# Two more PSUM banks for the hidden products of a two-layer MLP, and new due times for its weight conversions

## The chip, the cores and the metric

The kernel runs on one core of one Trainium2 chip. The metric is device time in microseconds (us), the median of several executions; one more execution is recorded by the hardware profiler, and the rows below come from it.

## The reference, cut to what matters

Attention with mixed heads gives `x` of 1792 tokens x 768; two layers follow it, and the change lies mostly in them:

```
h = x @ moe_w_in             # 1792 x 2048
g = s * relu(h)**2 + b
x = g @ moe_w_out            # 1792 x 768
h = x @ moe2_w_in
g = h * cos(h)
out = g @ moe2_w_out
```

All of it is float32. The kernel splits each operand into a high part that the fast matmul format holds exactly and a low rest, and adds three products: high x high, high x low, low x high.

## The kernel before, in words

**A plan, and then in-order queues.** The program is first a list of steps. Each step has a due position `pos`, an engine, a cost, steps it comes after, and tiles that it takes or uses. `Plan.run` walks through planned time: an engine that is free takes the step with the smallest `pos` that is ready and whose tiles are free in the plan. The order that comes out is the order in which each engine's instructions are written. On the chip every engine runs its own list in that order and waits at an instruction until its semaphores are up. So a due time or a cost changes no work, only the order on the queues of PE, DVE, ACT, POOL and SP.

**The attention** runs first. Per tile it does on PE the mix `p` (lines 457 to 459), then a maximum on DVE (468), the exponential `e` on ACT (475), weights `w` on DVE (488), the second mix `a` on PE (498) and its copy `at`. For each of eight half batches three pairs of products `vps` (535) with the values follow; they are copied to `xo` and stored to `x` in DRAM. `AVC` is the cost that the plan gives to one of the 48 steps of `vps`.

**The layers.** A layer's 2048 hidden columns are cut into eight slices of 256 (`f`), a slice into two halves of 128 (`c`). The tokens are cut into four blocks `j` of 512, 512, 256 and 512. A unit is a slice with a token block. `hidden` makes the 18 products of a half into one PSUM bank `h` (line 778 before, 779 after), `output` adds the unit's share of `g @ w_out` through PSUM banks `o` (line 841 in layer 1, 869 in layer 2; 842 and 870 after) into `acc` in SBUF (line 848 and 878 on DVE). PE's due order is: hidden of unit u+1, then output of unit u. In layer 2 a unit's output is made in blocks of 128 tokens, two banks and 12 products a block.

**What holds a hidden bank.** In layer 2 a half's bank is read by ACT (`ta`, 807), written and read again by DVE and ACT as scratch (811, 813, 815), and read last by the sine on ACT (`tb<-h`, 816). Only then may PE start another half in this bank. Before, there are two such banks (`ph`, one per half), and six for the output (`po`).

**Weights.** Each of a slice's four weight tiles (`weight(n, c, o)`: input weights `wi` with o=0, output weights `wo` with o=1) is loaded as float64 in two pieces, and each piece is split on ACT (700, 720), DVE (702, 707, 709, 714, 724) and POOL (726, 728) into `wh` and `wl`. The due times of these steps are given from `a`, the due time of the second unit of the slice before. `TOK` and `WT0` are the same for the tokens (`tokens`, 753 and 754) and the first slice's weights; `TAIL` places the layers behind the attention.

Of the kernel before, what the change touches and what calls it, by code (L numbers as in the profile page):

```python
# [10 lines left out]
F32 = mybir.dt.float32  # L11
# [6 lines left out]
PSUM = bass.MemoryType.PSUM  # L18
# [547 lines left out]
SHI = 16  # L566
OFF = (4.214, 4.208, 3.018, 2.518, 2.061, 1.245)
AVP = (2.713, 3000.0)
AVC = 900.0
W1 = (-1.242, 4.569)  # L570
W2 = (-1.416, 6.158)
W3 = (2.491, 1.454)
# [2 lines left out]
def mlp(pl, tc, x, w1, wo1, s, b, w2, wo2, out, left, right, psl, psr, bank, room, room_free, stored, gates, t_start):  # L575
# [6 lines left out]
    NF = DFF // 256  # L582
# [5 lines left out]
        t0 += n  # L588
    NB = len(TB)
    before_right, before_psr, before_left = gates  # L590
    for name, cap in (("raw2", 2), ("cm", 2), ("ca", 2), ("ce", 2), ("wi", 3), ("wo", 4), ("ta", 2), ("tb", 2), ("g0", 2), ("g1", 2), ("ph", 2), ("po", 6)):
        pl.ring(name, cap)
    P = {}

# [2 lines left out]
    for j in (0, 1):  # L597
        for z in range(2):
            for k in range(KD):
                n = TB[j][1]  # L600
# [35 lines left out]
    def open_left():  # L636
        left.close()
        psl.close()
        pool = lambda name, bufs=1: left.enter_context(tc.tile_pool(name=name, bufs=bufs, reuse_waits="tile"))
        P["po"] = psl.enter_context(tc.tile_pool(name="m_po", bufs=6, space=PSUM, reuse_waits="tile"))  # L640
        P["g"], P["wo"], xp = pool("m_g", 2), pool("m_wo", 4), pool("m_y")
        for j in (2, 3):
            for z in range(2):
                xx[z, j] = xp.tile([128, KD, TB[j][1]], F32R, name=f"x{z}{j}")
        for j in range(NB):
            acc[j] = xp.tile([128, KD * TB[j][1]], F32, name=f"acc{j}")
# [3 lines left out]
    g_psr = pl.add(t_start - 20000, "none", 0, open_psr, behind=before_psr)  # L650
    g_left = pl.add(t_start, "none", 0, open_left, behind=before_left + [g_right, g_psr])
# [8 lines left out]
    units = [(st, f, j) for st in range(2) for f in range(NF) for j in ((0, 1, 3, 2) if (st, f) == (1, NF - 1) else range(NB))]  # L660
    seq = [(st, f) for st in range(2) for f in range(NF)]
    cyc = lambda n: n / 2.4 + 13.5
# [11 lines left out]
    wt, w_done = {}, {}  # L674
# [85 lines left out]
    def hidden(u):  # L760
        st, f, j = u
        n = TB[j][1]
        nn = seq.index((st, f))
        for c in range(2):
            first = u == units[0]
            ring, tag = ("ps", "s") if first else ("ph", "h")
            hp = pl.hold(ring)
            p = at_h[u] + c * 18 * cyc(n)
            hw = wt[nn, c, 0]
            a = None  # L770
            for z in range(3):
                def prod(z=z, hp=hp, hw=hw, first=first, tag=tag):
                    if z == 0:
                        hp.tile = (bank if first else P["ph"]).tile([128, 512], F32, tag=tag, name="h")[:, :n]
                    for k in (2 * z, 2 * z + 1):
                        wh, wl = hw.tile[0][:, k], hw.tile[1][:, k]
                        for y, (w, z_) in enumerate(((wh, 0), (wh, 1), (wl, 0))):
                            nc.tensor.matmul(out=hp.tile, lhsT=w, rhs=cols(z_, j, k)[:, 0], start=(k == 0 and y == 0), stop=(k == KD - 1 and y == 2))  # L778
                xd = x_done[j][2 * z:2 * z + 2] if st == 0 else x_done[1, j]
                a = pl.add(p + z * 6 * cyc(n), "pe", 6 * cyc(n), prod, w_done[nn, c, 0] + xd + [a] + ([] if first else [g_psr]), take=[] if z else [hp], use=[hw])  # L780
            h_first.append(a)
            hg, h1, h2 = pl.hold(f"g{c}"), pl.hold("ta"), pl.hold("tb")
            gt[u, c] = hg
            p += 18 * cyc(n)
            act = n * .84 + 52
            dve = n * 1.05 + 66
            dp = 1000.0

            def open_t(h, tag):
                h.tile = P["t"].tile([128, 512], F32, tag=tag, name=tag)[:, :n]  # L790
                return h.tile

            def open_g(hg=hg, c=c):
                hg.tile = [P["g"].tile([128, 512], F32R, tag=f"{z}{c}", name=z)[:, :n] for z in ("gh", "gl")]
                return hg.tile[0]
            if st == 0:
                a = pl.add(p, "act", act, lambda h1=h1, hp=hp, open_t=open_t: nc.scalar.activation(out=open_t(h1, "ta"), in_=hp.tile, func=AF.Relu), [a], take=[h1], use=[hp])
                if first:
                    early.append(a)
                a = pl.add(p + dp, "dve", dve + 64, lambda h1=h1, h2=h2, open_t=open_t: nc.vector.scalar_tensor_tensor(  # L800
                    out=open_t(h2, "tb"), in0=h1.tile, scalar=P["sc"][:, 0:1], in1=h1.tile, op0=ALU.mult, op1=ALU.mult), [a] + c_sb, take=[h2], use=[h1], port=True)
                a = pl.add(p + 2 * dp, "act", act + 90, lambda h2=h2, open_g=open_g: nc.scalar.activation(
                    out=open_g(), in_=h2.tile, func=AF.Identity, bias=P["sc"][:, 1:2]), [a, g_left], take=[hg])
                a = pl.add(p + 3 * dp, "dve", dve + 64, lambda h2=h2, hg=hg: nc.vector.scalar_tensor_tensor(
                    out=hg.tile[1], in0=h2.tile, scalar=P["sc"][:, 1:2], in1=hg.tile[0].bitcast(F32), op0=ALU.add, op1=ALU.subtract), [a], use=[h2], port=True)
            else:
                a = pl.add(p, "act", act, lambda h1=h1, hp=hp, open_t=open_t: nc.scalar.activation(out=open_t(h1, "ta"), in_=hp.tile, func=AF.Copy), [a], take=[h1])
                a = pl.add(p + dp, "dve", n * .52 + 69, lambda h1=h1, h2=h2, open_t=open_t: nc.vector.tensor_scalar(
                    out=open_t(h2, "tb"), in0=h1.tile, scalar1=1.0 / (2 * math.pi), scalar2=MAGIC, op0=ALU.mult, op1=ALU.add), [a], take=[h2], port=True)
                a = pl.add(p + 2 * dp, "act", act + 90, lambda h2=h2: nc.scalar.activation(out=h2.tile, in_=h2.tile, func=AF.Identity, bias=P["cb"][:, 1:2]), [a])  # L810
                a = pl.add(p + 3 * dp, "dve", dve, lambda h1=h1, h2=h2, hp=hp: nc.vector.scalar_tensor_tensor(
                    out=hp.tile, in0=h2.tile, scalar=-C1, in1=h1.tile, op0=ALU.mult, op1=ALU.add), [a], port=True)
                a = pl.add(p + 4 * dp, "dve", dve, lambda h2=h2, hp=hp: nc.vector.scalar_tensor_tensor(
                    out=hp.tile, in0=h2.tile, scalar=-C2, in1=hp.tile, op0=ALU.mult, op1=ALU.add), [a])
                a = pl.add(p + 5 * dp, "act", act, lambda hp=hp: nc.scalar.activation(out=hp.tile, in_=hp.tile, func=AF.Abs), [a])
                a = pl.add(p + 6 * dp, "act", act + 90, lambda h2=h2, hp=hp: nc.scalar.activation(  # L816
                    out=h2.tile, in_=hp.tile, func=AF.Sin, scale=-1.0, bias=P["cb"][:, 0:1]), [a], use=[hp])
                a = pl.add(p + 7 * dp, "pool", n * 2.4 + 100, lambda h1=h1, h2=h2: nc.gpsimd.tensor_tensor(out=h2.tile, in0=h1.tile, in1=h2.tile, op=ALU.mult), [a], use=[h1])  # L818
                a = pl.add(p + 8 * dp, "act", act + 40, lambda h2=h2, open_g=open_g: nc.scalar.activation(out=open_g(), in_=h2.tile, func=AF.Copy), [a], take=[hg])
                a = pl.add(p + 9 * dp, "dve", dve, lambda h2=h2, hg=hg: nc.vector.tensor_tensor(out=hg.tile[1], in0=h2.tile, in1=hg.tile[0].bitcast(F32), op=ALU.subtract), [a], use=[h2], port=True)  # L820
            g_done[u, c] = a
# [61 lines left out]
    for n in range(len(seq)):  # L883
        if n == 0:
            for i, (c, o) in enumerate(((0, 0), (1, 0), (0, 1), (1, 1))):
                weight(0, c, o, t_start + WT0[i], t_start + WT0[i] + 6000)
            continue
        prev = [at_h[u] for u in units if u[:2] == seq[n - 1]]
        a = prev[1]
        weight(n, 0, 0, a, a + 12000)  # L890
        weight(n, 0, 1, a + 12000, a + 24000)
        weight(n, 1, 0, prev[3] + 18 * cyc(512), prev[3] + 18 * cyc(512) + 9000)
        weight(n, 1, 1, prev[3] - 8000, prev[3] + 3000)
    h_first = []
    for j in (0, 1):
        tokens(j, t_start + TOK[j][0], TOK[j][1])
    for i, u in enumerate(units):
        if u == units[2]:
            for j in (2, 3):
                tokens(j, t_start + TOK[j][0], TOK[j][1])  # L900
        hidden(u)
# [14 lines left out]
        pl.run()  # L916


TOK = ((-16000.0, 3835.4), (-1854.7, 2701.8), (6127.9, 1261.9), (11457.4, 1085.7))
WT0 = (-11637.0, -9965.5, 3371.0, 3000.0)  # L920
TAIL = 13954.5

# [1 line left out]
_INS = ["q", "k", "v", "w_pre", "w_post", "moe_w_in", "moe_w_out", "moe_s", "moe_b", "moe2_w_in", "moe2_w_out"]  # L924
# [23 lines left out]
```

## Time and profile before

| | |
|---|---|
| median of 3 executions | 1492.1 us (1489.51 to 1493.28) |
| profiled execution | 1494.0 us, span of its instructions 1492.2 us |
| PE busy | 1437.1 us, 96% of the span |
| DVE, ACT, POOL busy | 1210.2, 765.7, 626.4 us |
| attention until its last mix `p` ends | to 515.57 us |
| layer 1, first output to last hidden product before layer 2 | 557.83 to 994.16 us |
| layer 2, from its second hidden unit | 1002.34 to 1487.77 us |

The span is what the profile's instructions cover; the profiled time is 1.8 us longer than it. PE is busy nearly all the time, so what is to be read is where it is idle, and where its granted clock is below 1.00.

### The profile page before, as it was taken

Reading aid. Unit: us, or ns where it says so; the run is one execution under the profiler, and the core shown is the slowest. Engines: PE = TensorE matmul, PEld = TensorE weight load, DVE = VectorE, ACT = ScalarE, POOL = GpSimd, SP = SyncE. Lnnn points to the kernel's source line nnn. Section 1 sums busy time; section 2 is a strip of 40 time slices with the busy share of each in tenths; the row PEclk is TensorE's granted clock in tenths of the full one; section 3 lists DMA queues with packets and bytes.
Section 4 is the critical chain, followed back from the end, with each engine's and each line's share of the span. In section 5 each row is a group of like instructions: output and inputs, shape, how many; then the busy total and the mean of one; then the engine's idle time right before and its main releaser. Section 6 shows DMA issues by size and latency. Waiting matters only on the chain.

```text
span 1492.2 us, 23095 instructions
## 1 busy us (share of the span) xinstructions
PE 1437.1 (96%) x8292; PEld 1247.8 (84%) x8292; DVE 1210.2 (81%) x2212; ACT 765.7 (51%) x1595; POOL 626.4 (42%) x548
## 2 busy tenths in 40 slices
PE   6899999999999899999999999999999999999998
PEld 5788888887888778888888888889889898898988
DVE  4777777877877879898877877899899888988855
ACT  4766676666766746332323322357645445454532
POOL 2544454444444534443332333324454454454521
PEclk9999999999999999999999999999999999999999
DMA  6744464463454442221211212111211111111103
GB/s 175 159 129 134 110 157 129 133 144 109 126 128 132 138 135 74 75 64 54 74 45 51 64 43 64 43 46 50 64 54 43 54 53 54 53 44 53 54 30 118
DMA packets 140860, 129.19 MB, mean 87 GB/s; under 512 B 72171, under 2 KB 128459, under 8 KB 140747
## 3 DMA queue, kind: packets, MB, share of 16 engines
q1 hardware_dynamic: 140747, 127.73, 30.3%
q8 instruction: 65, 1.06, 0.3%
q14 instruction: 48, 0.39, 0.1%
HBM read 77.99 MB, written 11.01 MB: 60 GB/s over the span
## 4 chain that ended last, share of the span: by engine, by line
PE 85%; DMA 5%; DVE 4%; ACT 2%; issue 2%; SPq 1%; POOL 1%; DVEq 0%; POOLq 0%; ACTq 0%
PE h L778 30%; PE o L841 16%; PE o L869 15%; PE a L498 7%; PE vps L535 5%; DMA m<-s 3%; PE p L457 2%; PE sps L379 2%; PE sps L380 2%; PE p L459 2%; PE p L458 2%; PE tk L302 1%; PE tq L339 1%; DMA qn<-in_q_dram 1%; DVE w L488 1%
## 5 line engine op out<-in xcount | busy, mean ns | idle before, releaser
L726 POOL TENSOR_TENSOR cm<-ca,wh 128x384 f32<-128x384 f32 x128 | 168.6, 1319 | 387.8 <-ACT wh L720 387.8
L452 POOL TENSOR_TENSOR m<-m,mh 120x448 fp32r<-120x448 f32 x180 | 207.5, 1156 | 207.6 <-ACT mh L447 205.2
L778 PE MATMUL h<-m,wh 128*128 128x512 f32 x672 | 220.4, 398 | 12.4 <-ACT tb L816 12.4
L498 PEld LDWEIGHTS a<-w,e 120*128 120x128 f32 x1440 | 185.1, 194 | 21.0 <-PE p L459 6.5
L498 PE MATMUL a<-w,e 120*128 120x120 f32 x1440 | 189.8, 279 | 9.5 <-DVE w L488 9.5
L778 PE MATMUL h<-x,wh 128*128 128x256 f32 (+1 forms) x768 | 190.2, 339 | 2.2 <-DVE x L754 2.2
L728 POOL TENSOR_TENSOR wl<-cm,ce 128x384 fp32r<-128x384 f32 x128 | 150.2, 1175 | 70.3 <-DVE ce L724 64.6
L778 PEld LDWEIGHTS h<-m,wh 128*128 128x128 f32 x672 | 126.8, 191 | 42.3 <-ACT tb L816 15.6
L778 PE MATMUL h<-m,wl 128*128 128x512 f32 x384 | 152.0, 396 | 0.0
L778 PEld LDWEIGHTS h<-x,wh 128*128 128x128 f32 x768 | 131.9, 188 | 20.2 <-DVE x L754 2.6
L841 PE MATMUL o<-gl,wh 128*128 128x512 f32 (+1 forms) x384 | 140.1, 365 | 0.0
L841 PE MATMUL o<-gh,wh 128*128 128x512 f32 (+1 forms) x384 | 140.0, 365 | 0.0
L841 PE MATMUL o<-gh,wl 128*128 128x512 f32 (+1 forms) x384 | 140.0, 365 | 0.0
L475 ACT ACTIVATE e<-p,st 120x448 f32<-120x448 f32 x180 | 113.9, 633 | 36.8 <-DVE st L468 35.2
L778 PE MATMUL h<-x,wl 128*128 128x512 f32 (+1 forms) x384 | 130.0, 338 | 0.0
L468 DVE TENSOR_REDUCE st<-p 120x1 f32<-120x448 f32 x180 | 110.3, 615 | 23.3 <-PE p L459 22.9
L818 POOL TENSOR_TENSOR tb<-ta,tb 128x512 f32<-128x512 f32 (+1 forms) x64 | 76.0, 1187 | 118.1 <-ACT tb L816 111.6
L447 ACT ACTIVATE mh<-m 120x448 fp32r<-120x448 f32 x151 | 87.2, 577 | 66.1 <-PE p L458 43.9
L720 ACT ACTIVATE wh<-ca 128x384 fp32r<-128x384 f32 x128 | 66.0, 521 | 96.5 <-DVE ca L709 71.8
L878 DVE TENSOR_TENSOR acc<-acc,o 128x384 f32<-128x384 f32 x196 | 100.6, 544 | 17.3 <-PE o L869 17.1
L869 PE MATMUL o<-wh,gh 128*128 128x384 f32 x448 | 113.8, 334 | 0.0
L869 PE MATMUL o<-wh,gl 128*128 128x384 f32 x448 | 113.8, 334 | 0.0
(99 smaller groups left out, 3255.6 us busy)
## 6 DMA issues: line engine op xcount, KB each, us to landing
m<-s SPq DMA_DIRECT2D x144, 192.5 KB
raw<-in_moe_w_in_dram SPq DMA_DIRECT2D x64, 384.0 KB
raw<-in_moe_w_out_dram SPq DMA_DIRECT2D x64, 384.0 KB
qn<-in_q_dram SPq DMA_DIRECT2D x72, 110.0 KB
m<-s SPq DMA_DIRECT2D x36, 210.0 KB
v<-in_v_dram SPq DMA_DIRECT2D x28, 192.0 KB
out_dram<-acc SPq DMA_DIRECT2D x14, 384.0 KB
rk<-in_k_dram SPq DMA_DIRECT2D x18, 224.0 KB
```

The source lines that it names most:

```text
L447: nc.scalar.activation(out=hh.tile, in_=src().bitcast(F32), func=AF.Copy)
L452: a2 = pl.add(p - OFF[1] * STEP, "pool", 1110, lambda hh=hh, src=src: nc.gpsimd.tensor_tensor(out=src(), in0=src().bitcast(F32), in1=hh.ti ...
L468: nc.vector.tensor_reduce(out=hst.tile[:, 0, z:z + 1], in_=hp.tile, axis=AX, op=ALU.max, negate=True)
L475: nc.scalar.activation(out=he.tile, in_=hp.tile, func=AF.Exp, bias=hst.tile[:, 0, z:z + 1], accum_out=hst.tile[:, 1, z:z + 1])
L498: nc.tensor.matmul(out=ha.tile[:, c * L:(c + 1) * L], lhsT=he.tile[:, j:j + 128], rhs=hw2.tile[:, z], start=True, stop=True)
L726: a = pl.add(p0 + 6 * dp, "pool", 1050, lambda hm=hm, ha=ha, flat=flat: nc.gpsimd.tensor_tensor(out=hm.tile, in0=ha.tile.bitcast(F32), in1 ...
L728: got.append(pl.add(p0 + 7 * dp, "pool", 1050, lambda hm=hm, he=he, flat=flat: nc.gpsimd.tensor_tensor(out=flat(1), in0=hm.tile, in1=he.ti ...
L778: nc.tensor.matmul(out=hp.tile, lhsT=w, rhs=cols(z_, j, k)[:, 0], start=(k == 0 and y == 0), stop=(k == KD - 1 and y == 2))
L818: a = pl.add(p + 7 * dp, "pool", n * 2.4 + 100, lambda h1=h1, h2=h2: nc.gpsimd.tensor_tensor(out=h2.tile, in0=h1.tile, in1=h2.tile, op=ALU ...
L841: nc.tensor.matmul(out=hp.tile, lhsT=w, rhs=x, start=(c == 0 and y == 0), stop=(c == 1 and y == 2))
L869: nc.tensor.matmul(out=hp[e].tile, lhsT=x, rhs=w[:, e * HD:(e + 1) * HD], start=(c == 0 and y == 0), stop=(c == 1 and y == 2))
L878: got.append(pl.add(p, "dve", 470, lambda e=e, hp=hp, view=view: nc.vector.tensor_tensor(out=view(), in0=view(), in1=hp[e].tile, op=ALU.ad ...
```

## The change

```diff
-AVC = 900.0
+AVC = 1750.0
...
-("ph", 2), ("po", 6)):
+("ph", 2), ("pi", 2), ("po", 4)):
...
-        P["po"] = psl.enter_context(tc.tile_pool(name="m_po", bufs=6, space=PSUM, reuse_waits="tile"))
+        P["po"] = psl.enter_context(tc.tile_pool(name="m_po", bufs=4, space=PSUM, reuse_waits="tile"))
+        P["pi"] = psl.enter_context(tc.tile_pool(name="m_pi", bufs=2, space=PSUM, reuse_waits="tile"))
...
-            ring, tag = ("ps", "s") if first else ("ph", "h")
+            ring, tag = ("ps", "s") if first else ("ph", "h") if units.index(u) % 2 else ("pi", "i")
...
-        hp.tile = (bank if first else P["ph"]).tile([128, 512], F32, tag=tag, name="h")[:, :n]
+        hp.tile = (bank if first else P[ring]).tile([128, 512], F32, tag=tag, name="h")[:, :n]
...
-   w_done[nn, c, 0] + xd + [a] + ([] if first else [g_psr]), take=[] if z else [hp], use=[hw])
+   w_done[nn, c, 0] + xd + [a] + ([] if first else [g_psr] if ring == "ph" else [g_left]), take=[] if z else [hp], use=[hw])
...
-        weight(n, 0, 0, a, a + 12000)
-        weight(n, 0, 1, a + 12000, a + 24000)
-        weight(n, 1, 0, prev[3] + 18 * cyc(512), prev[3] + 18 * cyc(512) + 9000)
-        weight(n, 1, 1, prev[3] - 8000, prev[3] + 3000)
+        for i, (c, o) in enumerate(((0, 0), (0, 1), (1, 0), (1, 1))):
+            weight(n, c, o, a + WN[n > NF][i][0], a + WN[n > NF][i][1])
...
-TOK = ((-16000.0, 3835.4), (-1854.7, 2701.8), (6127.9, 1261.9), (11457.4, 1085.7))
-WT0 = (-11637.0, -9965.5, 3371.0, 3000.0)
-TAIL = 13954.5
+TOK = ((-16000.0, 1599.1), (-1854.7, -4153.7), (6127.9, -940.2), (11457.4, 2394.5))
+WT0 = (-11637.0, -6972.4, 3371.0, 1170.1)
+TAIL = 13826.2
+WN = (((500.1, 12000.0), (12000.0, 24676.0), (35989.2, 45236.9), (26000.0, 31685.4)), ((979.7, 12000.0), (11251.3, 24000.0), (32000.0, 39901.4), (20648.0, 31850.6)))
```

The output gives up two of its six banks. They become a second pair for the hidden products: even units (token blocks 0 and 2) use `pi`, odd ones `ph`. No product, conversion or load is added or taken away; the plan orders them anew. The order of three places matters below.

ACT, layer 2, around the turn from one slice to the next; before, `h_13488` is the second half of the last unit of a slice and `h_13569` the first half of the first unit of the next:

```order
L720 ACTIVATE wh_13520<-ca_13576 128x384
L807 ACTIVATE ta_13605<-h_13569 128x512
L815 ACTIVATE h_13488<-h_13488 128x512
L816 ACTIVATE tb_13560<-h_13488,cb_5760 128x512
L700 ACTIVATE cm_13631<-raw_13609 128x384
L819 ACTIVATE gh_13633<-tb_13560 128x512
```

The sine of `h_13488` stands behind the copy of `h_13569`. The same place after the change; `h_13396` and `h_13481` are the two halves of the last unit, `h_13567` is the first half of the next slice:

```order
L816 ACTIVATE h_13396<-h_13396 128x512
L817 ACTIVATE tb_13532<-h_13396,cb_5760 128x512
L820 ACTIVATE gh_13604<-tb_13532 128x512
L721 ACTIVATE wh_13550<-ca_13586 128x384
L808 ACTIVATE ta_13609<-h_13567 128x512
L701 ACTIVATE cm_13621<-raw_13577 128x384
L816 ACTIVATE h_13481<-h_13481 128x512
L817 ACTIVATE tb_13537<-h_13481,cb_5760 128x512
```

The sine of the first half now stands ahead of the copy of `h_13567`; that of the second half still stands behind it.

PE at the same turn, before: the end of `h_13569` and the start of the second half of the same unit, whose bank is that of `h_13488`:

```order
L778 MATMUL h_13569<-m_117,wh_13053 128x512 x2
L778 MATMUL h_13569<-m_117,wl_13054 128x512
L778 MATMUL h_13569<-m_117,wh_13053 128x512 x2
L778 MATMUL h_13569<-m_117,wl_13054 128x512
L778 MATMUL h_13617<-m_117,wh_13520 128x512 x2
L778 MATMUL h_13617<-m_117,wl_13521 128x512
```

After, behind `h_13567`:

```order
L779 MATMUL h_13567<-m_117,wh_13082 128x512 x2
L779 MATMUL h_13567<-m_117,wl_13083 128x512
L779 MATMUL h_13597<-m_117,wh_13082 128x512 x2
L779 MATMUL h_13597<-m_117,wl_13083 128x512
L779 MATMUL h_13597<-m_117,wh_13082 128x512 x2
```

Behind the first half of unit 0 there now comes `h_13597`, the first half of unit 1 with the same weights, in the bank of `h_13396`; the second half of unit 0 follows it, in a bank of the other pair.

PE where the attention ends, before: the last mix `p`, the last two pairs of `a`, the products `vps`, and the first hidden half `h_6180`:

```order
L459 MATMUL p_6070<-m_117,wp_h_114 120x448
L498 MATMUL a_6083<-w2_6075,e_6033 128x120 x4
L498 MATMUL a_6093<-w2_6075,e_6046 128x120 x4
L498 MATMUL a_6122<-w2_6116,e_6067 128x120 x4
L498 MATMUL a_6130<-w2_6116,e_6098 128x120 x4
L535 MATMUL vps_6143<-at_118,v_119 64x220 x16
L535 MATMUL vps_6167<-at_118,v_119 64x220 x8
L778 MATMUL h_6180<-m_117,wh_5914 128x512 x2
```

After, from the last mix on:

```order
L459 MATMUL p_6075<-m_117,wp_h_114 120x448
L498 MATMUL a_6093<-w2_6086,e_6032 128x120 x4
L498 MATMUL a_6099<-w2_6086,e_6053 128x120 x4
L779 MATMUL h_6107<-m_117,wh_5906 128x512 x2
L779 MATMUL h_6107<-m_117,wl_5907 128x512
L779 MATMUL h_6107<-m_117,wh_5906 128x512 x2
L779 MATMUL h_6107<-m_117,wl_5907 128x512
L779 MATMUL h_6107<-m_117,wh_5906 128x512 x2
L779 MATMUL h_6107<-m_117,wl_5907 128x512
L779 MATMUL h_6107<-m_117,wh_5906 128x512 x2
L779 MATMUL h_6107<-m_117,wl_5907 128x512
L498 MATMUL a_6139<-w2_6136,e_6073 128x120 x4
```

Twelve of the 18 products of the first hidden half have moved in between the last two pairs of `a`.

## Rows read from the trace of the kernel before

**Rows 1.** The page: busy time, share of the span, instructions

```profile
PE 1437.1 (96%) x8292; PEld 1247.8 (84%) x8292; DVE 1210.2 (81%) x2212; ACT 765.7 (51%) x1595; POOL 626.4 (42%) x548
```

**Rows 2.** Waits of PE, whole span: us in total, times, longest

```profile
PE h L778 <- ACT tb L816: 12.4, 7, 2.3
PE a L498 <- DVE w L488: 9.5, 15, 2.1
```

**Rows 3.** Busy time by window: a slice of layer 1, then three of layer 2

```profile
core 0: us, PE busy (x) PEld busy (x) DVE busy (x) ACT busy (x) POOL busy (x), PEclk, DMA share, GB/s
786.89:844.86 57.97, 57.97 (x290) 49.11 (x289) 46.30 (x81) 17.36 (x32) 19.11 (x16) 1.00 0.18 55
1184.57:1245.02 60.45, 58.55 (x313) 53.61 (x313) 52.37 (x100) 30.26 (x56) 30.09 (x24) 1.00 0.18 53
1245.02:1307.07 62.05, 60.15 (x313) 54.73 (x313) 54.76 (x102) 30.44 (x56) 30.70 (x24) 0.97 0.17 52
1429.58:1487.77 58.19, 58.19 (x325) 54.93 (x323) 33.36 (x63) 21.39 (x38) 9.22 (x8) 1.00 0.21 83
```

**Rows 4.** The same view, sum over the eight slices of layer 2

```profile
sum 485.43, PE 472.99 PEld 432.02 DVE 409.47 ACT 246.23 POOL 218.34; mean PE 59.12 PEld 54.00 DVE 51.18 ACT 30.78 POOL 27.29
```

**Rows 5.** Chain that ended last, around 1300 us: start, us, what

```profile
1290.87 4.19 PE o L869 x24
1295.06 4.14 PE h L778 x18
...
1299.22 0.60 ACT ta L807
1299.82 0.50 ACT h L815
...
1300.34 0.70 ACT tb L816
...
1301.08 5.99 PE h L778 x18
```

**Rows 6.** Timeline of ACT before that wait

```profile
1299.22 0.60 ACT L807 ACTIVATE ta<-h 128x512 f32<-128x512 f32 x1 [2.90 <-PE h L778]
```

**Rows 7.** Windows of PE from two such waits on: us, busy, clock

```profile
1238.70:1245.02 6.32, 4.42 (x20) 1.00 0.15 53
1299.20:1307.07 7.87, 5.99 (x19) 0.78 0.15 50
```

**Rows 8.** Output of one unit of layer 2: chain of PE, timeline of DVE

```profile
1213.66 8.33 PE o L869 x48
...
1216.43 1.00 DVE L878 TENSOR_TENSOR acc<-acc,o 128x384 f32<-128x384 f32 x2
...
1219.55 1.93 DVE L878 TENSOR_TENSOR acc<-acc,o 128x384 f32<-128x384 f32 x4
```

**Rows 9.** Timeline of POOL: last conversion of a slice's second input weights

```profile
1237.34 1.02 POOL L728 TENSOR_TENSOR wl<-cm,ce 128x384 fp32r<-128x384 f32 x1 [0.56 <-DVE ce L724]
```

**Rows 10.** Windows of PE where the attention ends: us, busy, clock

```profile
515.57:519.65 4.08, 2.02 (x17) 1.00 0.70 238
519.65:523.95 4.30, 3.63 (x16) 0.60 0.51 175
553.36:557.83 4.47, 2.29 (x15) 0.94 0.28 87
557.83:567.46 9.63, 9.63 (x37) 0.85 0.29 83
```

**Rows 11.** Chain and waits at the same place

```profile
528.63 2.95 PE h L778 x12
...
571.67 8.16 PE o L841 x36
...
PE h L778 <- DVE x L754: 2.2, 2, 1.1
```

**Rows 12.** Windows in the attention: two with `vps`, one between

```profile
90.00:130.00 40.00, 39.42 (x304) 32.87 (x303) 30.98 (x62) 26.14 (x59) 15.44 (x16) 1.00 0.45 126
160.00:190.00 30.00, 30.00 (x233) 24.47 (x232) 22.02 (x48) 16.30 (x38) 11.96 (x11) 1.00 0.50 119
190.00:215.00 25.00, 22.50 (x149) 19.30 (x149) 17.68 (x37) 17.86 (x43) 11.81 (x11) 1.00 0.64 161
```

**Rows 13.** Chain in the attention: one group of `vps`

```profile
96.84 1.70 PE vps L535 x16
```

More of the change, by code (lines that the diff above doesn't have):

```diff
@@ L590, in mlp @@
     before_right, before_psr, before_left = gates
-    for name, cap in (("raw2", 2), ("cm", 2), ("ca", 2), ("ce", 2), ("wi", 3), ("wo", 4), ("ta", 2), ("tb", 2), ("g0", 2), ("g1", 2), ("ph", 2), ("po", 6)):
+    for name, cap in (("raw2", 2), ("cm", 2), ("ca", 2), ("ce", 2), ("wi", 3), ("wo", 4), ("ta", 2), ("tb", 2), ("g0", 2), ("g1", 2), ("ph", 2), ("pi", 2), ("po", 4)):
         pl.ring(name, cap)
@@ L771, in hidden, with prod @@
             for z in range(3):
-                def prod(z=z, hp=hp, hw=hw, first=first, tag=tag):
+                def prod(z=z, hp=hp, hw=hw, first=first, ring=ring, tag=tag):
                     if z == 0:
-                        hp.tile = (bank if first else P["ph"]).tile([128, 512], F32, tag=tag, name="h")[:, :n]
+                        hp.tile = (bank if first else P[ring]).tile([128, 512], F32, tag=tag, name="h")[:, :n]
                     for k in (2 * z, 2 * z + 1):
@@ L779, in hidden @@
                 xd = x_done[j][2 * z:2 * z + 2] if st == 0 else x_done[1, j]
-                a = pl.add(p + z * 6 * cyc(n), "pe", 6 * cyc(n), prod, w_done[nn, c, 0] + xd + [a] + ([] if first else [g_psr]), take=[] if z else [hp], use=[hw])
+                a = pl.add(p + z * 6 * cyc(n), "pe", 6 * cyc(n), prod, w_done[nn, c, 0] + xd + [a] + ([] if first else [g_psr] if ring == "ph" else [g_left]), take=[] if z else [hp], use=[hw])
             h_first.append(a)
```

## The prediction

> **What bounds the kernel now.** I read the page's busy line first: PE is busy 1437.1 us, 96% of the span, and the next engine, DVE, 81% [rows 1]. So a change that takes no work from PE can at most take back PE's idle time, 1492.2 - 1437.1 = 55 us, and what a granted clock below 1.00 makes its work longer. Second, the waits of PE: two lines matter, hidden products that wait for the sine on ACT (7 times, 12.4 us), and mixes `a` that wait for weights from DVE (15 times, 9.5 us) [rows 2]. Third, windows by stage say where these stand. A slice of layer 1 has no idle time at all: 57.97 us, all of it busy, clock 1.00. Slices of layer 2 take 60.45 and 62.05 us, and the last one, which has no turn to a next slice in it, 58.19 [rows 3]. Over the eight slices of layer 2 the sum is 485.43 us, of which PE is busy 472.99 [rows 4]: 12.4 us idle, which is all of the waits for the sine. A slice at full clock holds 58.55 us of work [rows 3], eight of them 468.4; the other 472.99 - 468.4 = 4.6 us are work at a lower clock. So layer 2 holds 17.0 us that are not work, and layer 1 nothing.
>
> **Why PE waits there.** The chain at 1300 us shows the loop: PE ends the first half of unit 0 of the new slice (18 products, 4.14 us), then ACT makes `ta` (0.60), a second pass (0.50) and the sine `tb` (0.70), and only then PE starts the second half [rows 5]. The sine reads the bank that this half wants, the one of the last unit's second half. It could have run before, but in ACT's list it stands behind `ta` of the new unit, and ACT itself was idle for 2.90 us waiting for PE to end that half [rows 6]. ACT waits for PE, then PE for ACT: 0.60 + 0.50 + 0.70 and a few hundredths, 1.90 us in the window from 1238.70 (6.32 - 4.42) and 1.88 in that from 1299.20 (7.87 - 5.99) [rows 7].
>
> The second effect is in the same two windows. After the first wait the products take 4.42 us at clock 1.00, after the second 5.99 at 0.78 (some of it at the lower level): 1.57 us more. 4.6 / 1.57 is about 3, so about three of the seven waits are followed by such a fall.
>
> **The change in layer 2: the turn.** In the new order the bank that PE asks for behind the first half of unit 0 is that of the last unit's first half, whose sine stands ahead of `ta` in ACT's list; ACT can run it while PE makes the 4.14 us of unit 0. The bank of the second half, whose sine still stands behind `ta`, is asked for only another 18 products or more later; 0.60 + 0.50 + 0.70 = 1.8 us is covered by 4.14. The second half of unit 0 goes to the other pair. So no order is left in which both engines wait for each other, and I take the whole loss back: -12.4 of waits, and -4.6 of clock, since in the windows of before the clock falls only behind a wait: **-17.0**. At worst nothing comes back (0).
>
> What is late next? The second half's weights `wl`: POOL ends the last conversion at 1237.34 + 1.02 = 1238.36, 0.34 us before PE would have asked for them without its wait (1238.70) [rows 9]. With the old due times the removed wait would soon meet this one. Now that half is asked for 18 products later (+4.1 us), and its conversions are also due earlier. I cost it at nothing; with that cover gone it is at most the old wait less the 0.34 us, 1.6 us a turn or 11 in all.
>
> **Four output banks.** A block of an output takes two banks and 12 products, so four banks hold two blocks: the third block waits until DVE has added the first. In the trace of before one unit's 48 products take 8.33 us from 1213.66, 2.08 a block; blocks start at 1213.66, 1215.74, 1217.82 and 1219.91. The adds of the first block end at 1216.43 + 1.00 = 1217.43, 0.4 us before the third block; those of the second are two of the four that start at 1219.55, so they end at about 1220.5, 0.6 after the fourth would start [rows 8]. Six banks hide this, four do not, if DVE keeps this order. In the new order of PE there are three places per slice where only one block lies between two users of a bank; elsewhere hidden products stand between. The bounds are 0 (DVE's list is written anew with four banks known, and DVE has 58.55 - 52.37 = 6.2 us to spare per slice [rows 3]) and 3 x 0.6 = 1.8 us a slice, 14 in all. I take a quarter, 0.45 a slice, because of the three places only the kind of the fourth block is late in these rows, and the spare time exceeds the lateness threefold: 8 x 0.45 = **+3.6**. For layer 1 I take 0: DVE has 57.97 - 46.30 = 11.7 us to spare there [rows 3]; its upper bound is the same +3.6. And since PE never waits in layer 1, extra hidden banks can give it nothing.
>
> **From the attention to layer 1.** Windows show PE idle 4.08 - 2.02 = 2.06 us behind the last `p`, then 4.30 - 3.63 = 0.67, and 2.18 us in the first output; and 16 products that take 3.63 us at clock 0.60, against 2.02 for 17 at 1.00, 1.6 more; then 9.63 us at 0.85 for 37 [rows 10] where a full output of 36 takes 8.16 [rows 11], 1.4 more. In all 2.06 + 0.67 + 2.18 + 1.6 + 1.4 = 7.9 us. The change puts 12 hidden products between the last two pairs of `a`, 2.95 us [rows 11], more than the first wait. Against it: the last exponentials stand behind conversions on ACT's list, and the tokens' loads and conversions are due anew, while waits for them already cost 2.2 us [rows 11], so part may reappear later. Bounds 0 and -7.9, and I take the middle: **-4.0**.
>
> **The plan's cost of `vps`.** A group of 16 takes 1.70 us on PE [rows 13], 48 of them. The plan had 0.9 for it and now has 1.75. This only moves other steps about. Where `vps` stand in the mix, PE is busy 39.42 of 40 us and 30.00 of 30; between such places 22.50 of 25 [rows 12]. So there is little for a better plan to take near `vps`; the 9.5 us of `a` waiting for weights [rows 2] lie at the places that the new cost does not name. I take **0**, and as bounds a third of that 9.5 either way, 3 us.
>
> **Sum.** -17.0 + 3.6 + 0 - 4.0 + 0 = -17.4 us. The profiled execution took 1494.0 us (span 1492.2), so it would come to 1476.6. It is 1.9 above the median of the runs; the median goes from 1492.1 to **1474.7**.
>
> **The rivals.**
>
> *The wait moves.* The turn loses its loop, but PE meets the next late thing: adds on DVE, or `wl` from POOL, or token loads at the start of layer 1. For it speaks the 0.34 us that the weights had in hand [rows 9] and the fourth block's lateness [rows 8]. Against it: DVE and POOL are at 52 and 30 of 60 us in a slice [rows 3]. With the layer's gain halved (-8.5 + 3.6) and the transition at -4.0: -8.9, so 1483.2.
>
> *It does nothing.* If `ta` and `tb`, each with two buffers, still tie ACT's list to PE, the seven waits stay; then -4.0 + 3.6 = -0.4, 1491.7. Against it is the order: the sine of the bank now asked for stands ahead of the `ta` that waits.
>
> *Slower: short waits that bring the clock down.* If four banks make PE stop for about 0.6 us inside outputs, and each stop is followed by a fall as behind three of the seven waits, a stop costs 0.6 + 1.57 = 2.2 us. Two a slice make 8 x 2 x 2.2 = 35 us; with -17.0 and -4.0 that is +14, 1506. It decides from 21 / 8 = 2.6 us a slice on, a little over one such stop. Against it: four of the seven waits, of 1.9 us each, left the clock at 1.00 [rows 4, 7], and a stop of 0.6 is shorter than these.
>
> The Trainium skill, "TensorE: Matmul & The Clock Gate", section "A second HAM failure mode: psum-queue depth-cycling", speaks for this rival: it tells of a kernel that cycled through PSUM banks and in which PE was idle so often between groups of products that its clock went back and forth, and throughput fell. By it, fewer output banks are the thing not to do, and the sum would be the 1506 above. The trace of before agrees in part: falls follow some idle times of 1.9 us; no row of it shows one behind a stop inside an output.
>
> **How the numbers follow.** The forecast gets 0.65: its main term is a loop that the rows show in full and the new order opens. The moved wait gets 0.22, no effect 0.05, slower 0.08. For the range: the best case is all of layer 2, no price for banks, the whole transition and the attention's bound, -17.0 - 7.9 - 3 = -27.9, 1464; upward it takes in the moved wait with a margin of 4 for layer 1's and the attention's bounds, 1487. Above that lie no effect and slower, 0.13, and a little of the rest. About 0.3%, 4.5 us, is what a measurement of this kernel can tell from no change. Faster by more than this: the forecast and nearly all of the moved wait, 0.86; within it 0.06; slower 0.08.
>
> **What would show it.** Right: the line of `h` waiting for the sine is gone or below 2 us; slices of layer 2 take 58.5 to 59.5 us at clock 1.00; in ACT's timeline the sine of the first half ends before PE asks for its bank. The bank price right: `o` waits for DVE's adds in several short pieces, 2 to 6 us in all. The transition right: its idle time falls by about 2 us, and the first outputs run at a higher clock. Wrong: a new line of `h` waiting for `wl` or for `x`, of 8 us or more; waits of `o` for `acc` of over 1.8 us a slice; slices of layer 1 above 58.5 us; or windows of layer 2 with a clock below 0.95 and no long wait.

## The result and the profile after

| | before | after |
|---|---|---|
| median of 5 executions of each | 1492.16 us (1489.51 to 1494.7) | 1473.73 us (1471.07 to 1480.3) |
| ratio after / before | | 0.9874, 95% interval 0.9855 to 0.9894 |
| profiled execution, its span | 1494.0, 1492.2 us | 1480.3, 1478.5 us |
| granted clock over the span | 0.990 | 0.987 |

The forecast was 1474.7 us. The profiled execution is the slowest of the five, 6.6 us above the median, and has the lowest mean clock of them; the others have 0.991 to 0.995. So stages are compared below by PE's idle time and busy time apart, since a lower clock shows in the busy time alone. One later execution of the changed kernel, the one of that run that was profiled, took 3620 us and is left out of every comparison.

The page of the kernel after (busy time, share of the span, instructions):

```profile
PE 1432.6 (97%) x8292; PEld 1248.7 (84%) x8292; DVE 1211.6 (82%) x2228; ACT 756.9 (51%) x1580; POOL 614.2 (42%) x547
```

PE's waits in the kernel after, whole span (us in total, times, longest): the two largest, and those of hidden products:

```profile
PE p L457 <- ACT e L475: 11.2, 8, 3.2
PE a L498 <- DVE w L488: 6.6, 15, 1.0
...
PE h L779 <- DVE x L755: 0.8, 1, 0.8
...
PE h L779 <- ACT x L754: 0.4, 1, 0.4
```

The line with seven waits for the sine, 12.4 us [rows 2], is gone, and no line of outputs `o` waiting for DVE's adds has come. What has grown is a line of the attention: mixes `p` that wait for exponentials `e`, from 5.4 us before to 11.2.

Windows of the kernel after (columns as in [rows 3]): a slice of layer 1, three of layer 2, and layer 2 from its first hidden product to PE's end.

```profile
941.49:999.45 57.96, 57.96 (x290) 49.10 (x289) 52.76 (x91) 25.01 (x46) 17.93 (x14) 1.00 0.16 48
1174.24:1232.55 58.31, 58.31 (x313) 53.71 (x313) 53.98 (x101) 29.61 (x57) 27.73 (x25) 1.00 0.19 55
1232.55:1290.87 58.32, 58.32 (x314) 53.72 (x314) 53.99 (x101) 29.62 (x57) 28.27 (x25) 1.00 0.18 55
1290.87:1349.18 58.31, 58.31 (x314) 53.71 (x313) 53.94 (x101) 29.58 (x57) 27.63 (x25) 1.00 0.18 55
999.45:1474.23 474.78, 474.78 (x2534) 436.25 (x2532) 416.20 (x753) 247.10 (x470) 210.89 (x178) 1.00 0.18 57
```

The same stretch of layer 2 in the kernel before:

```profile
993.99:1487.94 493.95, 481.51 (x2534) 438.95 (x2532) 417.41 (x753) 249.09 (x470) 220.29 (x178) 0.99 0.17 54
```

Layer 1 is as it was, 57.96 us a slice. In layer 2 PE is now never idle: 474.78 of 474.78 us. It gains 493.95 - 474.78 = 19.17 us, of which 493.95 - 481.51 = 12.44 were idle and 481.51 - 474.78 = 6.73 were busy time.

How the turn looks now: ACT's timeline of the kernel after, then PE's, both around 1295 us, where a new slice begins at 1290.87.

```profile
1290.53 0.69 ACT L817 ACTIVATE tb<-h,cb 128x512 f32<-128x512 f32 x1
...
1295.19 0.60 ACT L808 ACTIVATE ta<-h 128x512 f32<-128x512 f32 x1 [0.78 <-PE h L779]
...
1296.75 0.69 ACT L817 ACTIVATE tb<-h,cb 128x512 f32<-128x512 f32 x1
```

```profile
1294.77 0.39 PE L779 MATMUL h<-m,wl 128*128 128x512 f32 x1
1294.99 0.62 PE L779 MATMUL h<-m,wh 128*128 128x512 f32 x2
```

ACT still waits for PE at `ta` (0.78 us), and a sine still stands behind that copy, the one at 1296.75. But the sine of the bank that PE takes next (by the order shown with the change, the one ahead of `ta`) ended at 1290.53 + 0.69 = 1291.22, 3.8 us before PE goes on without a pause at 1294.99.

How near the four output banks come to a wait: the place in layer 2 with the least in hand. A block fills two banks in turn, and its two adds free them in turn. Below are DVE's second add of a block, then PE's first two products two blocks later, and the second of them by itself, which takes the bank of that add.

```profile
1379.44 0.54 DVE L879 TENSOR_TENSOR acc<-acc,o 128x384 f32<-128x384 f32 x1
```

```profile
1380.21 0.51 PE L870 MATMUL o<-wh,gh 128*128 128x384 f32 x2
...
1380.38 0.33 PE L870 MATMUL o<-wh,gh 128*128 128x384 f32 x1
```

The add ends at 1379.98, the product starts at 1380.38: 0.40 us in hand, the least in the layer.

The front of the kernel, in windows up to the last mix `p` and from there to the first hidden product of layer 1's second slice (380 products in both kernels); first of the kernel before, then of the one after.

```profile
0.00:515.58 515.58, 482.08 (x3365) 409.56 (x3365) 389.50 (x783) 338.35 (x787) 235.76 (x230) 0.99 0.51 135
515.58:588.19 72.61, 67.67 (x380) 55.52 (x381) 61.04 (x103) 42.20 (x88) 30.22 (x25) 0.95 0.39 126
```

```profile
0.00:527.33 527.33, 488.07 (x3364) 416.18 (x3364) 395.25 (x798) 331.77 (x776) 238.39 (x230) 0.96 0.50 132
527.33:593.55 66.22, 63.84 (x380) 52.49 (x381) 59.85 (x102) 41.05 (x83) 26.19 (x21) 1.00 0.41 132
```

From the attention to layer 1 the kernel gains 72.61 - 66.22 = 6.39 us (2.56 of idle time, 3.83 of busy time, at a clock of 1.00 in place of 0.95). But the attention takes 527.33 - 515.58 = 11.75 us longer in this execution: 5.76 more idle, 5.99 more busy at a clock of 0.96 in place of 0.99. The account of the profiled execution: -19.2 - 6.4 + 11.8 and 0.1 in layer 1's other slices is -13.7, which is 1480.3 - 1494.0.

One place of that idle time stands on ACT, in the timeline of the kernel after:

```profile
498.89 0.55 ACT L701 ACTIVATE cm<-raw 128x384 f32<-128x384 f32 x1 [4.59 <-DMA raw<-in_moe_w_in_dram]
499.34 0.56 ACT L447 ACTIVATE mh<-m 120x448 fp32r<-120x448 f32 x1
499.81 0.62 ACT L475 ACTIVATE e<-p,st 120x448 f32<-120x448 f32 x1
```

ACT stands 4.59 us at the first conversion of layer 1's weights, whose load has not landed, and an exponential is queued behind it.

### The profile page after: what moved, and what is told of

Its sections match the earlier page's. It is cut to its first block, busy times and chain, and to the rows that moved or that the text cites. A ratio compares the mean times of both kernels' runs of the same rounds, so it can differ in the third digit from the quotient of the medians.

```text
span 1478.5 us, 23186 instructions
## 1 busy us (share of the span) xinstructions
PE 1432.6 (97%) x8292; PEld 1248.7 (84%) x8292; DVE 1211.6 (82%) x2228; ACT 756.9 (51%) x1580; POOL 614.2 (42%) x547
## 4 chain that ended last, share of the span: by engine, by line
PE 87%; DMA 5%; DVE 4%; ACT 1%; issue 1%; SPq 1%; POOL 1%; DVEq 0%; POOLq 0%; ACTq 0%
PE h L779 31%; PE o L870 16%; PE o L842 16%; PE a L498 8%; PE vps L535 5%; DMA m<-s 3%; PE p L457 2%; PE sps L379 2%; PE p L459 2%; PE sps L380 2%; PE p L458 2%; PE tk L302 1%; PE tq L339 1%; DVE st L468 1%; DMA qn<-in_q_dram 1%
## 5 line engine op out<-in xcount | busy, mean ns | idle before, releaser
L727 POOL TENSOR_TENSOR cm<-ca,wh 128x384 f32<-128x384 f32 x128 | 154.6, 1210 | 381.6 <-ACT wh L721 381.6
L779 PE MATMUL h<-m,wh 128*128 128x512 f32 x672 | 215.9, 391 | 0.0
L498 PEld LDWEIGHTS a<-w,e 120*128 120x128 f32 x1440 | 188.1, 197 | 19.0 <-PE p L459 9.1
L729 POOL TENSOR_TENSOR wl<-cm,ce 128x384 fp32r<-128x384 f32 x128 | 145.8, 1141 | 80.9 <-DVE ce L725 78.8
L819 POOL TENSOR_TENSOR tb<-ta,tb 128x512 f32<-128x512 f32 (+1 forms) x64 | 81.4, 1272 | 102.1 <-ACT tb L817 97.1
L870 PE MATMUL o<-wl,gh 128*128 128x384 f32 x448 | 113.8, 335 | 0.0
```

The costliest lines, as they stand in the source:

```text
L498: nc.tensor.matmul(out=ha.tile[:, c * L:(c + 1) * L], lhsT=he.tile[:, j:j + 128], rhs=hw2.tile[:, z], start=True, stop=True)
L727: a = pl.add(p0 + 6 * dp, "pool", 1050, lambda hm=hm, ha=ha, flat=flat: nc.gpsimd.tensor_tensor(out=hm.tile, in0=ha.tile.bitcast(F32), in1 ...
L729: got.append(pl.add(p0 + 7 * dp, "pool", 1050, lambda hm=hm, he=he, flat=flat: nc.gpsimd.tensor_tensor(out=flat(1), in0=hm.tile, in1=he.ti ...
L870: nc.tensor.matmul(out=hp[e].tile, lhsT=x, rhs=w[:, e * HD:(e + 1) * HD], start=(c == 0 and y == 0), stop=(c == 1 and y == 2))
```

## The experiments

Theory 1: the loss was the loop between ACT's list and PE at each turn; anything that opens the loop gains layer 2's part, and the output banks cost nothing. Rivals: (1) the new due times bring the gain; (2) a second pair of banks is needed whatever ACT's order; (3) four output banks have a price, in adds or in clock.

**Banks alone.**

The edit, against the kernel before, with `AVC` and `TOK` as they were there:

```diff
 AVC = 900.0
...
-("ph", 2), ("po", 6)):
+("ph", 2), ("pi", 2), ("po", 4)):
...
 TOK = ((-16000.0, 3835.4), (-1854.7, 2701.8), (6127.9, 1261.9), (11457.4, 1085.7))
```

> The second pair of banks and the four output banks, with all numbers (cost of vps, token, weight and tail due times) as before. Theory 1 (the loop between ACT and PE at the turn of a slice is the loss, and the second pair opens it): no wait of h for the sine, slices of layer 2 at 58.2 to 58.6 us, no wait of o for adds, in all 1472 to 1477 us. Rival 1 (the new due times bring the gain, the banks only allow them): waits stay or move to the weights wl, 1485 to 1492 us.

Measured: 1476.55 us, ratio 0.9878 (0.9856 to 0.9901). Layer 2 in windows, as above:

```profile
990.60:1465.90 475.30, 475.28 (x2534) 436.10 (x2532) 418.61 (x753) 247.90 (x470) 210.27 (x178) 1.00 0.19 57
```

Only 0.02 us of idle time is left with the old due times. The banks alone make layer 2's gain. The whole change had a ratio of 0.9874, so its new due times and its new cost add nothing to the banks that these runs can tell. In layer 2 they give some room: with the old due times three products start 0.05 us behind the end of the add that frees their bank, so there nothing is in hand, and the layer takes 0.5 us more than in the change.

**Numbers alone.**

```diff
-AVC = 900.0
+AVC = 1750.0
...
 ("ph", 2), ("po", 6)):
...
+TOK = ((-16000.0, 1599.1), (-1854.7, -4153.7), (6127.9, -940.2), (11457.4, 2394.5))
...
+WN = (((500.1, 12000.0), (12000.0, 24676.0), (35989.2, 45236.9), (26000.0, 31685.4)), ((979.7, 12000.0), (11251.3, 24000.0), (32000.0, 39901.4), (20648.0, 31850.6)))
```

> All new numbers, with two hidden and six output banks as before. Theory 1: the seven waits of about 1.9 us at the turns stay, slices of layer 2 at 60 to 62 us, in all 1488 to 1495 us. Rival 1: waits of h fall below 5 us in sum, 1474 to 1480 us.

Measured: 1496.17 us, ratio 1.0011 (0.9997 to 1.0025), 1.2 us above the range expected for theory 1. The wait of PE, and its windows up to the last `p` and on to layer 1's second slice:

```profile
PE h L778 <- ACT tb L816: 12.9, 7, 2.2
```

```profile
0.00:525.40 525.40, 485.79 (x3364) 411.76 (x3364) 395.15 (x798) 331.64 (x776) 237.93 (x230) 0.97 0.51 132
525.40:593.00 67.60, 64.25 (x381) 52.49 (x381) 60.41 (x103) 41.32 (x84) 29.34 (x22) 1.00 0.41 129
```

The seven waits stay. Rival 1 falls.

**The sine first.** No more banks; one dependence in the plan puts the sine ahead of the next unit's copy on ACT's list, PE's order staying as it was (some steps of DVE's list, and one of POOL's, shift with it).

```diff
-                a = pl.add(p, "act", act, lambda ...: nc.scalar.activation(..., func=AF.Copy), [a], take=[h1])
+                a = pl.add(p, "act", act, lambda ...: nc.scalar.activation(..., func=AF.Copy), [a] + (sine[-1:] if c == 0 else []), take=[h1])
...
+                sine.append(a)
```

> The kernel before with one more dependence in the plan: in layer 2 the copy ta of a unit's first half comes after the sine of the unit before, so that ACT's list has the sine ahead of it; banks, numbers and PE's order as before. Theory 1: the wait for the sine goes without any more banks, layer 2 gains 10 to 17 us; what may take its place is wl, which had 0.34 us in hand, at most 1.6 us a turn; 1475 to 1483 us. Rival 2 (two banks are too few whatever ACT's order, the second pair itself is needed): 1490 to 1494 us.

Measured: 1480.71 us, ratio 0.9901 (0.9878 to 0.9925). Its waits for the sine and its layer 2, then ACT at a turn:

```profile
PE h L779 <- ACT tb L817: 3.0, 5, 1.2
```

```profile
988.90:1468.40 479.50, 476.49 (x2534) 435.47 (x2532) 416.71 (x753) 248.87 (x470) 220.93 (x178) 1.00 0.18 56
```

```profile
1286.22 0.58 ACT L816 ACTIVATE h<-h 128x512 f32<-128x512 f32 x1 [2.70 <-DVE h L814]
1286.83 0.69 ACT L817 ACTIVATE tb<-h,cb 128x512 f32<-128x512 f32 x1
1287.42 0.59 ACT L808 ACTIVATE ta<-h 128x512 f32<-128x512 f32 x1
```

With ACT's order alone layer 2 gains 493.95 - 479.50 = 14.45 us of the 19.17. Rival 2 falls. What takes the place of the wait is not `wl`, as I expected, but DVE: the pass ahead of the sine comes late (ACT idle for 2.70 us at it), and PE waits 3.0 us in five pieces. The second pair of banks covers this too.

**Old front numbers with the new banks.**

```diff
-AVC = 1750.0
+AVC = 900.0
...
-TOK = ((-16000.0, 1599.1), (-1854.7, -4153.7), (6127.9, -940.2), (11457.4, 2394.5))
-WT0 = (-11637.0, -6972.4, 3371.0, 1170.1)
-TAIL = 13826.2
+TOK = ((-16000.0, 3835.4), (-1854.7, 2701.8), (6127.9, 1261.9), (11457.4, 1085.7))
+WT0 = (-11637.0, -9965.5, 3371.0, 3000.0)
+TAIL = 13954.5
```

> The changed kernel with cost of vps, token and first weight due times and the tail as before; the new banks and the new due times of later weights stay. Theory 1: layer 2 as after the change (58.3 us a slice). If the new numbers cost the attention its time (ACT's list waits for a weight's transfer with exponentials behind it): 1467 to 1472 us. If they gain at the start of layer 1 as forecast (4 us): 1476 to 1480 us.

Measured: 1477.45 us, ratio 0.988 (0.9853 to 0.9906). The median lies in the second expectation, but the six executions run from 1471.9 to 1481.0 us and so reach into both, and the ratio can't be told from the 0.9874 of the change: undecided.

**The cost of `vps` alone, and the change without it.**

```diff
-AVC = 900.0
+AVC = 1750.0
```

> The kernel before with only the plan's cost of a step of vps raised from 900 to 1750. Up to the second slice of layer 1, PE was idle 38.4 to 38.7 us in the three runs with the old front numbers and 41.6 to 43.0 in the two with the new ones. If the cost of vps makes the difference: 41 to 43.5 us here, and 1493 to 1499 us in all, the seven waits for the sine staying. If the due times of tokens and first weights make it: 38 to 39.3 us, 1490 to 1495 us.

```diff
-AVC = 1750.0
+AVC = 900.0
```

> The changed kernel with only the cost of vps set back to 900. If this cost makes the idle time ahead of layer 1's second slice: 38 to 39.3 us of it, 1470 to 1476 us. If the due times of tokens and first weights make it: 41 to 43.5 us, 1474 to 1480 us. Layer 2 as after the change, 474 to 476 us from its first hidden product to the end.

Measured: 1497.52 us, ratio 1.0022 (1.0008 to 1.0036), with the cost alone; 1480.72 us, ratio 0.9911 (0.9887 to 0.9935), for the change without it. The first is as expected if the cost matters, but the second is above both ranges that I gave (1470 to 1476 and 1474 to 1480). My figure of idle time up to layer 1's second slice told nothing apart: 42.7 and 41.5 us. Cut at the last `p` it does. Windows of the first kernel, then of the second:

```profile
0.00:524.30 524.30, 487.47 (x3364) 413.99 (x3364) 397.82 (x801) 332.16 (x777) 239.55 (x231) 0.97 0.51 133
524.30:597.60 73.30, 67.40 (x382) 54.76 (x382) 57.41 (x100) 40.80 (x85) 31.47 (x23) 0.95 0.38 119
```

```profile
0.00:512.90 512.90, 480.31 (x3364) 408.04 (x3364) 386.60 (x782) 336.22 (x784) 237.87 (x231) 0.99 0.52 134
512.90:592.10 79.20, 70.29 (x380) 57.98 (x381) 65.17 (x104) 42.84 (x87) 30.70 (x25) 0.89 0.38 120
```

Idle up to the last `p`: 36.8 us with the cost at 1750 alone, 32.6 with it back at 900. Behind it: 5.9 and 8.9, against 2.4 with the whole change. So the higher cost goes with more idle time in the attention, and the new due times make the way into layer 1 shorter only together with it. Setting the cost back does not make the changed kernel faster: what the attention saves is lost behind it, to idle time and to a clock of 0.89.

**Four output banks alone, with two hidden banks.**

```diff
-("ph", 2), ("po", 6)):
+("ph", 2), ("po", 4)):
...
-        P["po"] = psl.enter_context(tc.tile_pool(name="m_po", bufs=6, space=PSUM, reuse_waits="tile"))
+        P["po"] = psl.enter_context(tc.tile_pool(name="m_po", bufs=4, space=PSUM, reuse_waits="tile"))
```

> The kernel before with four output banks in place of six, and still two hidden banks (two banks unused). If four output banks cost nothing, since PE's list then has pieces of the next hidden half between the blocks: no wait of o for adds, the seven waits for the sine as before, 1490 to 1496 us. If they have the price that the forecast gave them, 0.45 us a slice: 1494 to 1500 us. If short stops bring the clock down: above 1505 us.

Measured: 1494.16 us, ratio 1.0003 (0.999 to 1.0016). The waits of hidden products for the sine, and the one wait of `o` for `acc`:

```profile
PE h L778 <- ACT tb L816: 12.6, 8, 1.9
...
PE o L869 <- DVE acc L878: 0.3, 1, 0.3
```

The median lies in two of my ranges, which overlap; the waits decide. Four output banks cost 0.3 us of waiting here, and nothing that the times can tell. The plan knew of them and wrote six-product pieces of the next hidden half between the blocks.

**Two output banks.**

```diff
-("ph", 2), ("pi", 2), ("po", 4)):
+("ph", 2), ("pi", 2), ("po", 2)):
```

> The changed kernel with two output banks in place of four: a block of 12 products starts only when the block before it has been added. An add ends about 1.4 us behind its block, six hidden products take as long, and the new order of PE still has about one pair of blocks a slice in layer 2 with nothing between. If stops of 0.5 to 1.5 us cost only themselves: 10 to 30 us of o waiting for adds over both layers, clock at 1.00 in layer 2, 1483 to 1505 us. If each such stop also brings the clock down: above 1510 us, with windows of layer 2 below 0.95. If pieces of hidden products cover all: 1472 to 1480 us.

Measured: 1506.66 us, ratio 1.0085 (1.0056 to 1.0115). Its waits in layer 2, its layer 2, and PE at one stop:

```profile
PE o L870 <- DVE acc L879: 10.8, 16, 1.1
...
PE h L779 <- ACT tb L817: 5.2, 5, 1.4
```

```profile
992.20:1498.40 506.20, 489.87 (x2558) 439.04 (x2556) 423.12 (x759) 246.24 (x475) 211.82 (x178) 1.00 0.18 54
```

```profile
1167.35 0.51 PE L870 MATMUL o<-wh,gl 128*128 128x384 f32 x2
1168.62 0.91 PE L870 MATMUL o<-wh,gh 128*128 128x384 f32 x2 [0.76 <-DVE acc L879]
```

The second of those two products by itself, and DVE's second add of the block before it:

```profile
1169.08 0.44 PE L870 MATMUL o<-wh,gh 128*128 128x384 f32 x1
```

```profile
1168.49 0.54 DVE L879 TENSOR_TENSOR acc<-acc,o 128x384 f32<-128x384 f32 x1
```

The time lies between my first two ranges. Now there are 21 stops, and the window of layer 2 is 506.20 - 474.78 = 31.4 us longer. Of this, 24 more output products of layer 1 that fall into the window (x2558 against x2534, 0.12 us apart) make 2.9, so the layer itself takes about 28.5 us more: 16.3 of idle time and about 12.2 of busy time, at a clock of 1.00 throughout. So short stops did not bring the clock down (rival 3's second half), but a stop costs more than the idle time that the profile shows. Part of that is waiting too. The first two products behind this stop take 0.91 us in place of 0.51, because the second waits again, for the block's second add: the add ends at 1168.49 + 0.54 = 1169.03 and the product starts at 1169.08, and the same 0.05 us lies between add and second product behind all 16 stops inside outputs. The profile counts this second wait as busy, since the first product is not yet at its end: about 0.29 us a stop, 4.5 in all. A further 0.16 us a stop, 3.4 in all, is the end of the last product ahead of the stop, which otherwise runs under the next one, and 0.1 a stop, 2.2 in all, are slower products behind it. This makes 10.1 of the 12.2; the other 2 have no single place in the trace.

**The changed kernel and the one with old front numbers on one chip.**

> The changed kernel once more, for a second profile and a comparison on the same chip with the other two of this group. Expected: idle time of PE up to the second slice of layer 1 again at 41 to 43 us, layer 2 at 474 to 476 us, 1472 to 1478 us. If the first profile's 41.6 us were an accident of one execution: 38 to 39.5 us.

> The changed kernel with the front numbers (cost of vps, token and first weight due times, tail) as before, once more, beside the changed kernel on the same chip. If the front numbers cost 3 us of idle time: PE idle 38 to 39.3 us up to the second slice of layer 1 and about 3 us faster than the changed kernel. If they cost nothing that a measurement can tell: within 2 us of it.

Measured: the changed kernel 1475.38 us, ratio 0.988 (0.9857 to 0.9903); with the old front numbers 1471.61 us, ratio 0.9852 (0.9828 to 0.9875). There is no profile of the first to compare, so its idle time stays untold. The windows of the second:

```profile
0.00:511.90 511.90, 479.61 (x3365) 407.31 (x3365) 389.52 (x783) 337.73 (x787) 235.31 (x230) 0.99 0.52 135
511.90:583.30 71.40, 65.73 (x382) 53.92 (x382) 58.98 (x100) 41.40 (x87) 27.33 (x22) 0.98 0.39 122
```

It is 3.8 us faster than the changed kernel by the medians, as expected if the front numbers cost idle time, and the idle time up to the last `p` is 32.3 us against 39.3 in the change's profile. Side by side on this chip the executions do not overlap (1468.6 to 1473.2 against 1474.3 to 1477.0 us). But the intervals of the two ratios do, and in its first run, on another chip, the same kernel had a ratio of 0.988, no better than the 0.9874 of the change; that this version beats the change is likely and not shown.

**The first weights' conversions behind exponentials.**

```diff
-            a = dma(p0 - 5000, load, part, 128 * PN * 8, [g_right], take=[hr])
+            a = dma(p0 - 5000, load, part, 128 * PN * 8 * (6 if (n, c, o) == (0, 0, 0) else 1), [g_right], take=[hr])
```

> The changed kernel, with the plan told that the first weight tile's two loads take six times as long. No load moves; on ACT's list the two conversions that wait for these loads come behind two and six more exponentials. If ACT's wait for the load (4.6 us, with exponentials queued behind) is what makes PE idle longer there: the waits of p for e fall from 11 to 5 to 7 us in sum, idle time up to the second slice of layer 1 to 36 to 39 us, 1468 to 1474 us. If not: 41 to 43 us as with the change, since then the later weights only shift the wait to the first hidden products.

Measured: 1475.7 us, ratio 0.988 (0.9856 to 0.9905), the same as the changed kernel beside it. ACT's timeline at the first conversion, the wait of PE, and the windows:

```profile
496.43 0.55 ACT L701 ACTIVATE cm<-raw 128x384 f32<-128x384 f32 x1
```

```profile
PE p L457 <- ACT e L475: 8.9, 9, 1.7
```

```profile
0.00:515.00 515.00, 479.44 (x3350) 408.59 (x3351) 391.58 (x795) 329.80 (x770) 234.19 (x228) 0.98 0.51 135
515.00:588.70 73.70, 67.46 (x398) 55.93 (x397) 64.63 (x110) 41.68 (x86) 32.06 (x24) 0.98 0.40 124
```

ACT's wait for the load is gone, and the idle time up to the last `p` falls from 39.3 to 35.6 us. But behind it the idle time is 6.2 in place of 2.4, so the sum, 41.8, is that of the change (41.6). (18 products have moved behind the last `p` here, so the two busy times don't compare with those of the change; the idle times do.) My theory that this wait costs the front its time falls: without it the idle time comes a step later.

## Why the prediction was right, step by step

**The turn** was right. The loop is the cause: it stays when only numbers change, gives back 14.45 of the 19.17 us when ACT's order is changed with no more banks, and goes wholly with the second pair. The term was -17.0 and the stretch gained 19.2. The mis-sized part is what I took for clean work: 58.55 us, from a slice of [rows 3] that has a wait in it, where a slice without one takes 58.31. The difference, 0.24 x 8 = 1.9 us, went with the waits. It fits two things in the lines below: the first two products behind the wait take 0.73 us, and 0.62 otherwise; and a product that takes 0.40 us is followed by the next after 0.23 (1241.20 and 1241.43), so the last one ahead of a wait shows about 0.16 us that otherwise run under the next.

```profile
1240.63 0.73 PE L778 MATMUL h<-m,wh 128*128 128x512 f32 x2 [1.90 <-ACT tb L816]
1241.20 0.40 PE L778 MATMUL h<-m,wl 128*128 128x512 f32 x1
1241.43 0.62 PE L778 MATMUL h<-m,wh 128*128 128x512 f32 x2
```

The prediction's "seven waits, of 1.9 us each" is not right: two took 1.26 us, four 1.90 and one 2.33. Its count of about three falls of the clock is: behind the wait of 2.33 and two of those of 1.90 the next 3.5 us ran at 0.52 to 0.60, behind the other four at 1.00.

**Four output banks** were forecast at +3.6 and cost no wait with the change and 0.3 us alone. The step that failed is reading DVE's lateness off the old lists: the plan wrote both lists anew with four banks, and in the change 0.40 us is the least in hand. With two banks the same mechanism costs layer 2 about 28.5 us, so the worry was sound, and the number of banks at which it sets in is below four.

**From the attention to layer 1** the term was -4.0 and the stretch gained 6.4 in the profiled execution, 3.8 of it busy time at a higher clock. This gain can't be parted from the next term: with the cost of `vps` set back the stretch takes 79.20 us.

**The plan's cost of `vps`** is where the prediction failed: "I take 0", within 3 us either way. I argued from PE's idle time where `vps` stand, and not from what else the new cost shifts. With the higher cost PE was idle 35.6 to 39.6 us up to the last `p` in the five profiles that have it, and 32.0 to 33.5 in the seven that don't. The means, 37.4 and 32.8, are 4.6 us apart. Up to layer 1's second slice PE was idle 36.9 to 38.7 us in the six profiles with all the front's numbers old, and 39.2 to 43.0 in the six with any of them new: all in all the front lost by the new numbers. In the change itself the waits of `p` for `e` grew by 5.8 us (11.2 from 5.4). These waits sum to 8.9 to 11.2 us in the four profiles that have both the new cost and the new due times, and to 4.5 to 5.9 in the other eight. Without ACT's wait for one load the idle time up to the last `p` was 3.7 less, and this came back behind the attention. In the kernel with the cost alone the waits of `p` for `e` hardly grew, so why its attention is idle longer stays open.

So the layers gave 5.8 us more than forecast (-19.2 in place of -13.4), and the front gave about that much less: by the medians, -18.4 + 19.2 = about +1 in place of -4.0. That the forecast time of 1474.7 came within 1 us is luck: two errors cancel. The mechanism that carries the result was the right one.

**The rivals.** That the wait moves to adds or `wl` did not happen in layer 2; it did in the experiment that has only ACT's order, to DVE. Slower by stops that bring the clock down: even 21 stops left it at 1.00 in layer 2. The Trainium skill, "TensorE: Matmul & The Clock Gate", section "A second HAM failure mode: psum-queue depth-cycling", puts the lost throughput of a kernel that cycled through PSUM banks down to its clock going back and forth. The two-bank kernel lost 28.5 us in layer 2 with no fall of the clock there, by the waits themselves and what stands beside them, so its loss is of another kind; the falls behind three of the seven waits of the kernel before agree with the section.

## What to carry to other kernels

Where two engines with in-order queues wait for each other once per turn, look in the other engine's list for what stands ahead of the step that is needed: moving that step gave 14 of the 19 us with no more buffers. A buffer taken from another ring can be free when the lists are written anew for the smaller ring and some work stands between its users, as with four output banks here and not with two; count what is in hand in the new order, not what is late in the old one. A planner's cost set nearer to the truth is a change of every list behind it, and its price shows stage by stage, with idle and busy time read apart.

## What the runs showed that I had not expected

A stop can hide part of its waiting in PE's busy time. Behind the 16 stops inside outputs of the two-bank kernel the second product waited again, 0.29 us or so, while the first was still running, and a profile that counts an engine as busy from a product's start to its end shows this as longer products. What a stop costs beside waiting was small: about 0.16 us ahead of it and 0.1 behind. And the clock did not fall in layer 2 behind any of these 21 stops, of 0.47 to 1.44 us, while it did behind three of the seven waits of 1.26 to 2.33 us before, and behind one of eight waits for the sine in the kernel with four output banks alone: a fall is no fixed price of a stop.
